# Two query blocks of values at the end of every second slot, in two output banks, in the last ten slots of a sliding-window attention

## The chip, the cores and the metric

The kernel runs on one core of one Trainium2 chip. The metric is the device time of one execution in microseconds (us). The engines are TensorE (PE in the profile; its weight loads are PEld), VectorE (DVE), ScalarE (ACT), GpSimd (POOL) and SyncE (SP), which issues the transfers. TensorE writes only to the accumulators, eight banks of 128 partitions by 512 float32 values.

## The reference

The input x is 2048 tokens of 512 values. It is normalised per token; the result feeds an attention with a window of 256 keys, 32 heads of 16 values, and a mixer with 1792 hidden units; the output joins them.

```python
xn = _layernorm(x)
qkv = (xn @ wqkv).reshape(B, S, 3, H, Dh)            # S 2048, H 32, Dh 16
scores = einsum("bhqd,bhkd->bhqk", q, k) * Dh ** -0.5
mask = (i - j >= 0) & (i - j < 256)
s = (softmax(where(mask, scores, -1e9)) @ v) @ wo
h = gelu(_layernorm(xn) @ w1 + b1)
return x + s * silu(h @ w2 + b2)
```

## The kernel before, in words

**Stages.** The attention stage is followed by a mixer stage that works through the tokens in four chunks of 512. The attention takes the heads four at a time (NQ is 8 groups) and the tokens in 16 blocks of 128, which makes 128 slots, counted by t in the loop at lines 818 to 850. Slot t stands for group t // 16 and block t % 16. Every engine executes its instructions in the order in which this loop records them (the class Ordered, lines 32 to 47), so the loop is a schedule written out by hand.

**One slot**, in the order in which TensorE gets it:

- `prob_block(n, kb, 1)` (lines 547 to 563) makes the scores of key block kb against the three query blocks that can see it, for two of the four heads, with two matmuls of up to 128x384 (`w` is 384, and 256 and 128 for the last two blocks of a group). From slot 116 on they go to the accumulator xy, which was needed until then for running maxima. ScalarE takes the exponential into a buffer `pt`, and GpSimd masks it with two affine selects.
- a first helping of filling matmuls into the banks fb (`fill_in(t, 0)`), and what the plan has for this slot
- `prob_block(n, kb, 0)`, the same for the other two heads, through the accumulator stb
- a second helping of filling matmuls (`fill_in(t, 1)`)
- `pv_step` (lines 568 to 581): the values of one query block, that of the slot before. The query block needs the probabilities of up to three key blocks, so it is 12 matmuls with 17 columns of weights (16 values and the sum), into four groups of rows of `otb`, which is columns 256 to 383 of the second bank of zo (line 194). ScalarE copies it to `oraw`; after four blocks a transfer writes `oraw` to oT_d in memory, from where the mixer stage reads it.

**What fills.** The filling matmuls of the last slots are hidden units of the first chunk (`pair_h`), two at a time in the two row halves of TensorE. `tandem` (lines 439 to 470) spreads them: units 12 and 13 over slots 116, 117, 119 and 120 with the rest in 121, units 2 and 3 over slots 122, 123, 125 and 126 with the rest in 127 (line 745). Slots 118 and 124 get none.

**Buffers.** `pt` comes from a pool of 8 buffers (line 64), two per key block, so four key blocks are held at once. zo is one tile of two banks (line 193). Until slot 115 its columns 0 to 255 take scores for the maxima (`first_scores`, lines 486 to 493); after that only `otb` is in use. The area with the tag `wa` in the pool bigp holds first weights, then an input chunk (`open_y`, line 588), and after the last slot the first hidden units (`activate_first`, line 785).

**After the last slot**, in slot 128 (lines 800 and 801): a hidden unit on all rows (`first_h(0)`), the values of block 127, a second hidden unit (line 856), and then the projections of the mixer stage.

Waits between engines are not written by hand: the recording layer sets them from what instructions read and write, as counts of semaphores.

Of the kernel before, what the change touches and what calls it, by code (L numbers as in the profile page):

```python
# [9 lines left out]
F32 = mybir.dt.float32  # L10
# [8 lines left out]
P = 128  # L19
# [31 lines left out]
def mixer_kernel(ctx, tc, x, wqk, wv, wo, w1, b1, w2, b2, out):  # L51


    nc = SimpleNamespace(**{name: Ordered(tc, name) for name in ("tensor", "vector", "scalar", "gpsimd", "sync")})

    const = ctx.enter_context(tc.tile_pool(name="const", bufs=1))
    bigp = ctx.enter_context(tc.tile_pool(name="bigp", bufs=1))
# [6 lines left out]
    pp = attn.enter_context(tc.tile_pool(name="pp", bufs=8))  # L64
# [95 lines left out]
    def run(steps):  # L160
        for step in steps:
            step()
# [13 lines left out]
    def open_slot(i):  # L176
        slots.append(bigp.tile([P, 2, 2, S], F32R, tag=f"qk{i}", name=f"qk{i}"))
# [5 lines left out]
    oT_d = dram.tile([4, 8, 32, S], F32, name="oT_d")  # L183
# [9 lines left out]
    zo = psum.tile([P, 2, 512], F32, name="zo")  # L193
    otb = zo[:, 1, 256:384]
# [291 lines left out]
    def first_scores(n, qb):  # L486

        slot = slots[n % 2]
        for p in range(2):
            for a in (1, 0):  # L490
                r = slice(64 * a, 64 * a + 64)
                nc.tensor.matmul(zo[:, a, P * p: P * (p + 1)], slot[r, 0, p, P * qb: P * (qb + 1)],
                                 slot[r, 1, p, P * (qb - 2): P * (qb - 1)], start=True, stop=True)

    def max_block(n, qb, ahead=False):

        slot = slots[n % 2]
        if qb % 4 == 0:
            mts[n, qb // 4] = small.tile([P, 2, 2, 4], F32, tag="mt", name=f"mt_{n}_{qb}")
        lo = max(qb - 1, 0)  # L500
        off = 128 * (lo + 1 - qb)
        for p in range(2):
            for a in (1, 0):
                r = slice(64 * a, 64 * a + 64)
                nc.tensor.matmul(xy[:, a, 256 * p + off: 256 * (p + 1)], slot[r, 0, p, P * qb: P * (qb + 1)],
                                 slot[r, 1, p, P * lo: P * (qb + 1)], start=True, stop=True)
        if qb >= 2 and not ahead:
            first_scores(n, qb)
        four = xy.rearrange("q a (p k) -> q a p k", p=2)
        nc.vector.copy_predicated(four[:, :, :, 128:256], mask,  # L510
                                  neg if qb < 2 else zo[:, :, 0:256].rearrange("q a (p k) -> q a p k", p=2))
        nc.vector.tensor_reduce(out=mts[n, qb // 4][:, :, :, qb % 4],
                                in_=four[:, :, :, off:256],
                                axis=AX.X, op=ALU.max, negate=True)

    def max_rows(n, c, t):

        mt = mts.pop((n, c))
        mh = small.tile([P, 2, 2, 2, 4], F32R, tag="mh", name=f"mh_{n}_{c}")
        apart = t >= 0  # L520
        eng = nc.gpsimd if apart else nc.vector
        eng.tensor_copy(mh[:, :, 0], mt)
        eng.tensor_tensor(mh[:, :, 1], mt, mh[:, :, 0].bitcast(F32), op=ALU.subtract)
        mT = small.tile([P, 32], F32, tag="mT", name=f"mT_{n}_{c}")

        def turn_rows():
            nc.vector.transpose(mT, mh.rearrange("p a l i b -> p (a l i b)").bitcast(F32))
        if apart:
            behind(t + 1, turn_rows)
        else:  # L530
            turn_rows()
        t += apart
        rows = mT_d[n, c]
        at(t + 1, nc.sync.dma_start, rows.rearrange("r (i t) -> i r t", i=4), mT)

        def bring_in():
            nc.sync.dma_start(slots[n % 2][3:P:32, 0, :, 512 * c: 512 * (c + 1)].bitcast(F32),
                              rows.rearrange("(h p b) t -> h p (b t)", h=4, p=2))
        if (n, c) == (6, 3):
            among[7, 3] = bring_in  # L540
        else:
            behind(t + 2, bring_in)


    pts = {}

    def prob_block(n, kb, p):
        slot = slots[n % 2]
        w = min(384, S - P * kb)
        pt = pp.tile([P, 2, 384], F32, tag="pt", name=f"pt_{n}_{kb}_{p}")  # L550
        both = xy if p and 16 * n + kb + LEAD >= 16 * NQ else stb[0]
        for a in (1, 0):
            r = slice(64 * a, 64 * a + 64)
            nc.tensor.matmul(both[:, a, 0:w], slot[r, 1, p, P * kb: P * (kb + 1)],
                             slot[r, 0, p, P * kb: P * kb + w], start=True, stop=True)
        nc.scalar.activation(pt[:, :, 0:w], both[:, :, 0:w], AF.Exp, scale=DH ** -0.5)
        nc.gpsimd.affine_select(out=pt[:, :, 0:P], in_=pt[:, :, 0:P], pattern=[[0, 2], [1, P]],
                                compare_op=ALU.is_ge, fill=0.0, base=0, channel_multiplier=-1)
        if w == 384:
            nc.gpsimd.affine_select(out=pt[:, :, 256:384], in_=pt[:, :, 256:384],  # L560
                                    pattern=[[0, 2], [-1, P]], compare_op=ALU.is_gt, fill=0.0,
                                    base=0, channel_multiplier=1)
        pts[(n, kb, p)] = pt


    outs = {}

    def pv_step(n, qb):

        lo = max(qb - 2, 0)  # L570
        for kb in range(lo, qb + 1):
            for j in range(4):
                nc.tensor.matmul(otb[32 * j: 32 * j + DH + 1], vt[:, kb, (4 * n + j) % 16],
                                 pts[n, kb, j // 2][:, j % 2, P * (qb - kb): P * (qb - kb + 1)],
                                 start=(kb == lo), stop=(kb == qb),
                                 skip_group_check=True, tile_position=(0, 32 * j))
        if qb % 4 == 0:
            outs[0] = sgp.tile([P, 512], F32, tag="or", name=f"oraw_{n}_{qb}", bufs=2)
        outs["copy"] = nc.scalar.copy(outs[0][:, P * (qb % 4): P * (qb % 4 + 1)], otb)
        if qb % 4 == 3:  # L580
            (at if n or qb > 7 else behind)(16 * n + qb + 2, nc.sync.dma_start, oT_d[n // 2, n % 2::2, :, P * (qb - 3): P * (qb + 1)], outs[0])


    mlp = {}
# [79 lines left out]
    def at(t, fn, *args):  # L664
        plan.setdefault(t, []).append((fn, args))
# [37 lines left out]
    n, raw = raws["qk"]  # L703
# [107 lines left out]
    def fill_in(t, half):  # L811
        now[:] = t, half
        run(delayed.pop((t, half), ()))
        for fn, args in fills.get((t, half), ()):
            fn(*args)

    end = 16 * NQ
    for t in range(-16, end + 1):
        m = t + LEAD
        if t == -5:  # L820
            open_slot(1)
            for k in range(4):
                at(-4 + k, clear_part, k)
        if 0 <= t < end:
            if t == 0:
                early.close()
                stb.append(attn.enter_context(tc.tile_pool(name="ps_s2", bufs=1, space=PSUM)).tile(
                    [P, 2, 512], F32, name="stb"))
            prob_block(t // 16, t % 16, 1)
        if t >= 0 and m < end:  # L830
            max_block(m // 16, m % 16, m not in IN_PLACE)
        fill_in(t, 0)
        for fn, args in plan.get(t, []):
            fn(*args)
        if 4 <= m < LEAD:
            max_block(0, m)
        if 0 <= t < end:
            prob_block(t // 16, t % 16, 0)
        fill_in(t, 1)
        if 0 <= m < 4:  # L840
            max_block(0, m)
        if t >= 0 and m + 1 < end and (m + 1) % 16 >= 2 and m + 1 not in IN_PLACE:
            first_scores((m + 1) // 16, (m + 1) % 16)
        if t >= 1:
            pv_step((t - 1) // 16, (t - 1) % 16)
        run(lns.get(t, ()))
        if 0 <= m < end and m % 4 == 3:
            max_rows(m // 16, m % 16 // 4, t)
        for fn, args in ends.get(t, []):
            fn(*args)  # L850
# [22 lines left out]
    for f in range(6, NF, 2):  # L873
        t = gp.tile([P, 2, 512], F32, tag="ohl", name=f"hr_{f}", bufs=4)
# [429 lines left out]
```

## Time and profile before

| what | value |
|---|---|
| time, median of 3 runs | 750.63 us (750.46 to 751.04) |
| the profiled execution's own time | 750.88 us |
| its span in the profile | 749.2 us |
| granted TensorE clock | 1.0 |
| the last ten slots, 403.86 to 425.79 us | 21.93 us |

The span is the time from the first to the last instruction that the profile shows; 1.7 us of the execution lie around it. A row of the timeline has the start in us, the duration, the engine, the line, the operation, the tile written and the tiles read, the shape, and how many equal instructions are merged; in brackets stands how long the engine was idle ahead of it and who released it. All instructions have line 43, because one helper records them, so tiles tell them apart: xy and stb are scores, fb is filling, zo the values, pt probabilities, oraw the copy of the values. TensorE overlaps matmuls, so durations in a row overlap; what a piece of work costs is read from start to start.

### The profile page before, as it was taken

How to read it: one execution, taken by the hardware profiler on the slowest of the kernel's cores; microseconds unless marked ns; L12 is line 12 of the kernel's file. 1: busy time of each engine (PE TensorE's matmuls, PEld its weight loads, DVE VectorE, ACT ScalarE, POOL GpSimd, SP SyncE). 2: the span in 40 equal slices, each digit the busy share in tenths (PEclk: the TensorE clock that was granted, in tenths of full speed). 3: DMA queues.
4: the chain of work that ended last, by engine and by line, in shares of the span. 5: the costliest groups of instructions: out<-in, count | busy, mean ns of one | idle time of the engine just before them, and what ended most of it. 6: DMA issues, size and time to landing. Idle time of an engine off the chain costs nothing.

```text
span 749.2 us, 18758 instructions
## 1 busy us (share of the span) xinstructions
PE 733.9 (98%) x7408; PEld 590.4 (79%) x7408; DVE 511.7 (68%) x781; ACT 441.1 (59%) x746; POOL 299.3 (40%) x644
## 2 busy tenths in 40 slices
PE   8999999999999999999999999999999999999997
PEld 7886777777778888777776788888888888888886
DVE  7886777877766778887872648763576765676743
ACT  7757767867667676778877745444463744442001
POOL 7413757767666555767877600120102000001102
PEclk9999999999999999999999999999999999999999
DMA  8633356766555535647724482542012232253611
GB/s 288 191 74 78 84 133 149 201 168 183 152 142 145 144 90 142 162 111 190 200 86 148 133 286 94 165 151 82 31 45 102 93 100 72 70 174 123 222 45 56
DMA packets 56951, 99.40 MB, mean 133 GB/s; under 512 B 11104, under 2 KB 11360, under 8 KB 56864
## 3 DMA queue, kind: packets, MB, share of 16 engines
q1 hardware_dynamic: 56864, 98.21, 45.7%
q8 instruction: 58, 0.95, 0.5%
q14 instruction: 29, 0.24, 0.1%
HBM read 51.39 MB, written 29.62 MB: 108 GB/s over the span
## 4 chain that ended last, share of the span: by engine, by line
PE 89%; ACT 5%; DVE 2%; POOL 2%; issue 1%; DMA 1%; SPq 0%; DVEq 0%; ACTq 0%; POOLq 0%
PE acc L43 20%; PE fb L43 18%; PE zo L43 11%; PE stb L43 9%; PE p L43 9%; PE s L43 6%; PE h L43 6%; PE xy L43 5%; ACT pt L43 4%; PE pv L43 3%; POOL pt L43 1%; DVE xy L43 1%; PE yt L43 1%; DMA x<-in_x_dram 1%; DVE mt L43 0%
## 5 line engine op out<-in xcount | busy, mean ns | idle before, releaser
L43 POOL TENSOR_SCALAR_AFFINE_SELECT pt<-pt 128x256 f32<-128x256 f32 x480 | 193.8, 428 | 132.9 <-ACT pt L43 131.7
L43 ACT ACTIVATE pt<-stb 128x768 f32<-128x768 f32 (+1 forms) x244 | 188.8, 774 | 62.4 <-PE stb L43 54.8
L43 DVE TENSOR_REDUCE mt<-xy 128x4 f32<-128x1024 f32 (+1 forms) x128 | 152.6, 1192 | 4.4
L43 DVE COPY_PREDICATED xy<-upper,zo 128x512 f32<-128x512 int32 x112 | 77.8, 695 | 70.6 <-PE xy L43 63.1
L43 POOL TENSOR_TENSOR xo<-xo,gated 128x512 f32<-128x512 f32 x15 | 20.3, 1358 | 216.8 <-DVE gated L43 192.9
L43 PE MATMUL fb<-xnT,wqb 64*128 64x512 f32 (+1 forms) x684 | 104.8, 397 | 0.3
L43 PE MATMUL zo<-pt,vt 128*17 128x128 f32 x2880 | 103.7, 275 | 0.3 <-POOL pt L43 0.3
L43 PE MATMUL stb<-qk 64*128 64x384 f32 (+1 forms) x488 | 97.2, 393 | 6.2 <-ACT pt L43 4.1
L43 PE MATMUL acc<-w,gh 128*128 128x512 f32 x320 | 98.9, 390 | 0.0
L43 PEld LDWEIGHTS stb<-qk 64*128 64x128 f32 x488 | 45.8, 183 | 51.6 <-ACT pt L43 46.6
L43 PEld LDWEIGHTS zo<-pt,vt 128*17 128x17 f32 x2880 | 67.5, 97 | 15.6 <-issue 6.3
L43 PEld LDWEIGHTS fb<-xnT,wqb 64*128 64x128 f32 (+1 forms) x684 | 64.7, 185 | 11.0 <-DVE pjr L43 1.4
L43 PEld LDWEIGHTS acc<-w,gh 128*128 128x128 f32 x320 | 59.8, 188 | 12.3
L43 PE MATMUL acc<-w,gl 128*128 128x512 f32 x160 | 62.4, 390 | 0.0
L43 PE MATMUL xy<-qk 64*128 64x256 f32 (+2 forms) x536 | 58.4, 291 | 0.2 <-DVE mt L43 0.2
L43 PEld LDWEIGHTS xy<-qk 64*128 64x128 f32 x536 | 46.7, 185 | 6.7 <-issue 3.1
L43 ACT COPY oraw<-zo 128x128 f32<-128x128 f32 x128 | 34.2, 267 | 29.2 <-PE zo L43 28.9
L43 ACT ACTIVATE gated<-acc 128x512 f32<-128x512 f32 x16 | 8.7, 596 | 65.6 <-DVE acc L43 65.6
L43 PE MATMUL s<-wos,ohl 128*128 128x512 f32 (+1 forms) x204 | 44.7, 378 | 0.0
L43 PEld LDWEIGHTS s<-wos,ohl 128*128 128x128 f32 x204 | 36.7, 188 | 7.2 <-DVE gated L43 0.2
L43 PEld LDWEIGHTS zo<-qk 64*128 64x128 f32 x448 | 38.5, 185 | 4.4 <-issue 1.4
L43 ACT COPY p<-p 128x512 f32<-128x512 f32 x21 | 12.3, 586 | 49.7 <-PE p L43 42.3
(195 smaller groups left out, 1241.5 us busy)
## 6 DMA issues: line engine op xcount, KB each, us to landing
qk<-sh SPq DMA_DIRECT2D x128, 128.0 KB
qk<-pjr SPq DMA_DIRECT2D x64, 128.0 KB
oT_d<-oraw SPq DMA_DIRECT2D x32, 256.0 KB
w_d<-in_w_dram SPq DMA_DIRECT2D x14, 512.0 KB
x<-in_x_dram SPq DMA_DIRECT2D x16, 256.0 KB
or<-oT_d SPq DMA_DIRECT2D x16, 256.0 KB
w<-rden_d SPq DMA_DIRECT2D x16, 256.0 KB
xo<-in_x_dram SPq DMA_DIRECT2D x16, 256.0 KB
```

The costliest lines, as they stand in the source:

```text
L43: r = issue(*args, **kwargs)
```

## The change

From slot 118 on, `pv_step` is called in odd slots only, for two query blocks: those of the slot two before and of the slot before (slot 119 does blocks 117 and 118, slot 127 does 125 and 126). Odd blocks use `otb` in the second bank as ever, even blocks the same columns of the first bank. Block 127 stays in slot 128. Because blocks of probabilities are now read up to one slot later, those of key blocks 118 and 123 get a buffer in the area `wa`, outside the pool of 8, one tile for both halves. The transfer of `oraw` is planned for the slot after the one in which the block is computed; so for blocks 116 to 119 and 120 to 123 it moves back by a slot.

```diff
+    TWOS, APART, spare = 118, (118, 123), []
     def prob_block(n, kb, p):
...
-        pt = pp.tile([P, 2, 384], F32, tag="pt", name=f"pt_{n}_{kb}_{p}")
+        if 16 * n + kb in APART:
+            if p:
+                spare.append(bigp.tile([P, 2, 2, 384], F32, tag="wa", name=f"pt_{n}_{kb}"))
+            pt = spare[-1][:, p]
+        else:
+            pt = pp.tile([P, 2, 384], F32, tag="pt", name=f"pt_{n}_{kb}_{p}")
...
-    def pv_step(n, qb):
+    def pv_step(n, qb, t):
+        otb = zo[:, int(t < TWOS or qb % 2), 256:384]
...
         if qb % 4 == 3:
-            (at if n or qb > 7 else behind)(16 * n + qb + 2, nc.sync.dma_start, oT_d[n // 2, n % 2::2, :, P * (qb - 3): P * (qb + 1)], outs[0])
+            (at if n or qb > 7 else behind)(t + 1, nc.sync.dma_start, oT_d[n // 2, n % 2::2, :, P * (qb - 3): P * (qb + 1)], outs[0])
...
-        if t >= 1:
-            pv_step((t - 1) // 16, (t - 1) % 16)
+        for q in range(t - 1, t) if t < TWOS or t == end else range(t - 2, t) if t % 2 else ():
+            if q >= 0:
+                pv_step(q // 16, q % 16, t)
```

## The prediction, as it was put on record

> **What bounds the kernel now.** I read the page first, then the chain of work that ended last, then the last slots of the attention in the timeline of all engines.
>
> ```profile
> span 749.2 us, 18758 instructions
> PE 733.9 (98%) x7408; PEld 590.4 (79%) x7408; DVE 511.7 (68%) x781; ACT 441.1 (59%) x746; POOL 299.3 (40%) x644
> ```
>
> The chain of waits from 425 us to the end, grouped by engine and line:
>
> ```profile
> by line: PE acc L43 47.1%; PE p L43 20.6%; PE s L43 13.6%; PE h L43 13.5%; PE fb L43 1.9%; PE yt L43 1.6%; PE zo L43 0.5%; DVE xo L43 0.3%; DVE gated L43 0.2%; issue 0.0%; PE stb L43 0.0%; DVEq L43 0.0%
> ```
>
> TensorE is busy for 98% of the span. Nearly all of that chain is matmuls that follow each other. So whatever the attention's last slots gain or lose, the end gains or loses, unless something waits there for another engine. The last ten slots are these (start, duration; PE is matmuls, PEld weight loads; each of the 12 matmuls of a block of values has two rows, so x24 is one block):
>
> ```profile
> 401.43 0.85 PE L43 MATMUL fb<-xnT 64*128 64x512 f32 x6
> 402.12 0.34 PE L43 MATMUL stb<-qk 64*128 64x384 f32 x2
> 402.29 0.86 PE L43 MATMUL fb<-xnT 64*128 64x512 f32 x6
> 403.08 0.85 PE L43 MATMUL zo<-pt,vt 128*17 128x128 f32 x24
> 403.86 0.44 PE L43 MATMUL xy<-qk 64*128 64x384 f32 x2
> 404.00 0.27 ACT L43 COPY oraw<-zo 128x128 f32<-128x128 f32 x1 [0.68 <-PE zo L43]
> 404.14 0.34 PE L43 MATMUL stb<-qk 64*128 64x384 f32 x2
> 404.41 0.57 PEld L43 LDWEIGHTS zo<-pt,vt 128*17 128x17 f32 x24 [0.25 <-ACT oraw L43]
> 404.41 0.85 PE L43 MATMUL zo<-pt,vt 128*17 128x128 f32 x24
> 404.43 0.81 ACT L43 ACTIVATE pt<-xy 128x768 f32<-128x768 f32 x1 [0.16 <-PE xy L43]
> 405.29 0.18 PEld L43 LDWEIGHTS xy<-qk 64*128 64x128 f32 x2 [0.31 <-ACT pt L43]
> 405.29 0.44 PE L43 MATMUL xy<-qk 64*128 64x384 f32 x2
> 406.76 0.85 PE L43 MATMUL zo<-pt,vt 128*17 128x128 f32 x24
> 407.54 0.45 PE L43 MATMUL xy<-qk 64*128 64x384 f32 x2
> ...
> 410.02 0.44 PE L43 MATMUL xy<-qk 64*128 64x384 f32 x2
> 411.27 0.85 PE L43 MATMUL zo<-pt,vt 128*17 128x128 f32 x24
> 411.76 0.83 ACT L43 ACTIVATE pt<-stb 128x768 f32<-128x768 f32 x1
> 412.05 0.44 PE L43 MATMUL xy<-qk 64*128 64x384 f32 x2
> 412.47 0.29 ACT L43 COPY oraw<-zo 128x128 f32<-128x128 f32 x1
> 414.76 0.45 PE L43 MATMUL xy<-qk 64*128 64x384 f32 x2
> 416.70 0.85 PE L43 MATMUL zo<-pt,vt 128*17 128x128 f32 x24
> 417.48 0.45 PE L43 MATMUL xy<-qk 64*128 64x384 f32 x2
> 417.62 0.27 ACT L43 COPY oraw<-zo 128x128 f32<-128x128 f32 x1 [0.69 <-PE zo L43]
> 418.03 0.63 PE L43 MATMUL zo<-pt,vt 128*17 128x128 f32 x16
> 418.98 0.41 PE L43 MATMUL zo<-pt,vt 128*17 128x128 f32 x8 [0.31 <-POOL pt L43]
> 419.32 0.44 PE L43 MATMUL xy<-qk 64*128 64x384 f32 x2
> 421.57 0.39 PE L43 MATMUL xy<-qk 64*128 64x256 f32 x2
> 423.95 0.33 PE L43 MATMUL xy<-qk 64*128 64x128 f32 x2
> 425.79 0.50 PE L43 MATMUL fb<-yh,xnT 128*128 128x512 f32 x1
> ```
>
> A slot opens with its scores in xy. The last one, slot 127, is 128 columns wide and opens at 423.95; counting back, slot 118 opens at 403.86, and the first hidden unit follows at 425.79. The ten slots take 21.93 us: 1.43, 2.25, 2.48, 2.03, 2.71, 2.72, 1.84, 2.25, 2.38 and 1.84. TensorE hardly stands still in them. Only slots 118 and 124 have no filling matmuls (fb), and there two waits show. The block of values at 404.41 waits for the copy of the block before (404.00 plus 0.27 is 404.27; the weight load waited 0.25). The scores at 405.29 wait for the exponential that still reads xy (404.43 plus 0.81 is 405.24).
>
> **The change part by part.** Unit prices, from start to start in the rows above: a block of values costs 0.78 (406.76 to 407.54). Six fb rows before scores take 0.69 (401.43 to 402.12), before a block of values 0.79 (402.29 to 403.08), so that turn costs 0.10. Scores after a block take 0.28 (403.86 to 404.14), after fb 0.17 (402.12 to 402.29), so the turn back costs 0.11. A block that follows another and waits for its copy starts 1.33 after it (403.08 to 404.41, and again 416.70 to 418.03): the copy starts 0.92 after the block, lasts 0.27, and 0.14 go to the release and the first weights.
>
> *Even slots lose their block.* In slots 120, 122 and 126 that is 0.78 and one turn of 0.10, 0.88 each: 2.48, 2.71 and 2.38 become 1.60, 1.83 and 1.50. The next scores need the exponential of this slot's first half, which ends 0.57 (403.86 to 404.43) plus 0.81 plus 0.05 after the slot opens, 1.43; it is still covered. Slots 118 and 124 have nothing but scores, and there the removed block was the cover of exactly this wait. So 118 stays at 1.43: its block leaves and an idle TensorE takes its place. Slot 124 falls from 1.84 to 1.43, which is what the wait for GpSimd's mask (418.98) and the copy had cost above the exponential. Sum: 3 times 0.88 plus 0.41, a gain of 3.05.
>
> *Odd slots get a second block.* That is 0.78 in each of the five, and the question on which the forecast hangs: does the second block wait for the copy of the first? The change puts it into the other bank of zo. But zo is one tile, and the instruction list of the changed kernel, built but not run, names a wait. In each pair the first matmul of the second block waits for ScalarE's counter at the copy that was issued just ahead, the first block's; the first block names no such wait any more. Nothing is left to fill that wait, since scores and fb stand before the pair. So the second block starts 1.33 after the first instead of 0.78, and each odd slot grows by 1.33: 6.65. Behind the waiting matmul stand, on TensorE, the rest of the block and the next slot's scores; for those waits ScalarE's next exponential, and for that GpSimd. Bounds of this wait: nothing, if the start could be taken at once (0.78 start to start), and 0.83 rather than 0.55 where the copy comes late on ScalarE. Slot 121 shows that late case: scores stand right ahead of the block, an fb copy and the exponential at 411.76 precede the copy, and it starts 1.20 after the block (411.27 to 412.47) instead of 0.92. The same order stays, so I add 0.28 there once. In slot 127 the exponentials are a third as wide, and I take 0.92. I take 0.55 elsewhere because two rows give 1.33 directly.
>
> *Turns.* Slots 121, 123 and 127 now open after fb or scores and not after a block: 3 times 0.11 gained. Slots 119 and 125 open after a wait, and I give them nothing.
>
> *What costs nothing.* The two blocks of probabilities outside the ring of eight need no wait: that area was last read by slots around 92, and its second use, in slot 123, comes after block 120 of values in slot 121. The other blocks find their ring buffer read a slot earlier, as before; block 120 takes that of block 115, last read by the first block of the pair in slot 119, and its exponential comes after the whole pair. If that failed, an exponential (0.81) would be late once. In the queue of SP the writes of blocks 116 to 119 and 120 to 123 are issued a slot later, the first now behind two writes of h_d. They are read a stage later, behind the last such write, which is not earlier either way. ScalarE gets both copies behind each other, ahead of the next slot's exponential, which needs scores that come after the second block anyway.
>
> Slot by slot this gives 1.43, 3.58, 1.60, 3.53, 1.83, 3.94, 1.43, 3.58, 1.50 and 3.06, together 25.48 against 21.93: **plus 3.55 us** (6.65 plus 0.28, less 3.05 and 0.33).
>
> *Does the rest take it up?* After 425.79 come two hidden units and the projections:
>
> ```profile
> 425.86 2.95 PE fb L43 x12
> 428.81 0.78 PE zo L43 x24
> 429.59 2.97 PE fb L43 x12
> 432.56 5.44 PE acc L43 x24
> ```
>
> All of it is TensorE, and what it reads next is made from the last slots' results, so it shifts with them. I count no refund. The profiled execution took 750.88 us with a span of 749.2; that execution would be at 754.4. It lies 0.25 above the median of 750.63, from which I forecast 754.2.
>
> **The rivals.**
>
> *The banks do stand apart.* If the second block started at once, the five waits of 0.55 and the 0.28 would fall away: 3.55 less 3.03 is plus 0.5, 751.2, not slower by anything that can be told here. It decides from a wait of about 0.2 per pair downward (0.5 and five times 0.2 is 1.5). For it speaks that the blocks write different banks, and that only the copy reads the first. Against it speak the wait in the built list and the two rows in which a block does stand for a copy. On this the Trainium skill, "PSUM — Partial Sum Buffer", section "Summary: rules for kernel authors", says that to read the accumulators while matmuls run, one should take a different bank, and guard by bank. By that rule this rival would be right, with its 751.2; no row of this trace shows a block written beside the copy of another bank of zo, so it neither agrees nor contradicts, and the rule says what the memory allows, not which waits were written into the program. Chance 0.07.
>
> *The copy is late in every pair.* If ScalarE reaches the copy as late as in slot 121 in the other four pairs too, that is 4 times 0.28, and if the turns saved don't show, 3 times 0.10 and 0.33 more: 3.55 plus 1.75, 755.9. For it speaks GpSimd:
>
> ```profile
> 405.30 3.06 POOL L43 TENSOR_SCALAR_AFFINE_SELECT pt<-pt 128x256 f32<-128x256 f32 x8 [1.15 <-ACT pt L43]
> 412.67 10.49 POOL L43 TENSOR_SCALAR_AFFINE_SELECT pt<-pt 128x256 f32<-128x256 f32 x19 [0.43 <-ACT pt L43]
> ```
>
> Its masks take 0.38 each at first and 0.55 later, four to a slot, so 2.2 us a slot; in a pair the second block needs those of the slot just before. Against it: over two slots that is 4.4 us, and the pairs of full width take 5.0 or more in the sum above. Chance 0.12.
>
> *The block was no cover in slots 118 and 124, and the banks stand apart.* Then 118 would save its 0.78 as well, and the sum is about plus 0.5 less 0.8, 750.4: no change that can be told, or a little faster. Against it is the row at 405.29, which names the exponential. Chance 0.02.
>
> **How the numbers follow.** The forecast has 0.79, the late copy 0.12, the separate banks 0.07, the last 0.02. A measurement of this kernel can tell about 0.2%, 1.5 us, from no change, so slower begins at 752.1. The range goes from 752.4, where three of the five waits fall away (1.65) and 0.15 more, to 755.9, the late copy; it leaves out the two rivals below. Slower: 0.79 and 0.12, less 0.01 for a forecast that is off by more, 0.90. Same: 0.08. Faster: 0.02.
>
> **What would show it.** In the profile after, TensorE's weight loads of zo should wait for "ACT oraw" five times for about half a us, in slots 119, 121, 123, 125 and 127, with two blocks 1.33 apart (1.6 in slot 121). The scores of slots 119 and 125 should wait some 0.8 for "ACT pt". The first hidden unit should start at about 429.3 instead of 425.79, and the distance from there to the end should stay. If the pairs stand 0.78 apart the wait was wrong; if slot 118 is shorter than 1.4 the cover was.

## The result and the profile after

The changed kernel takes 754.45 us (median of 6 runs, 753.88 to 754.96); the kernel before, run beside it, 750.62 (750.30 to 751.33). The ratio is 1.0049, 95% interval 1.0036 to 1.0062: slower by half a per cent. The profiled execution took 754.45 us with a span of 752.7, 3.5 more than before. The forecast was 754.2.

The last slots of the changed kernel in TensorE's timeline (start, duration, engine, what, and in brackets the idle time ahead and its releaser; slot 118 opens at 403.87, slot 127 at 426.15):

```profile
403.87 0.44 PE L43 MATMUL xy<-qk 64*128 64x384 f32 x2
404.15 0.34 PE L43 MATMUL stb<-qk 64*128 64x384 f32 x2
405.21 0.44 PE L43 MATMUL xy<-qk 64*128 64x384 f32 x2 [0.73 <-ACT pt L43]
...
406.68 0.85 PE L43 MATMUL zo<-pt,vt 128*17 128x128 f32 x24
407.92 0.85 PE L43 MATMUL zo<-pt,vt 128*17 128x128 f32 x24 [0.38 <-ACT oraw L43]
408.70 0.44 PE L43 MATMUL xy<-qk 64*128 64x384 f32 x2
...
410.31 0.34 PE L43 MATMUL xy<-qk 64*128 64x384 f32 x2
...
411.18 0.35 PE L43 MATMUL stb<-qk 64*128 64x384 f32 x2
411.46 0.85 PE L43 MATMUL zo<-pt,vt 128*17 128x128 f32 x24
413.26 0.85 PE L43 MATMUL zo<-pt,vt 128*17 128x128 f32 x24 [0.96 <-ACT oraw L43]
...
421.17 0.44 PE L43 MATMUL xy<-qk 64*128 64x384 f32 x2 [0.81 <-ACT pt L43]
...
426.15 0.23 PE L43 MATMUL xy<-qk 64*128 64x128 f32 x2
...
428.34 0.85 PE L43 MATMUL zo<-pt,vt 128*17 128x128 f32 x24 [0.39 <-ACT oraw L43]
429.12 0.50 PE L43 MATMUL fb<-yh,xnT 128*128 128x512 f32 x1
```

Every odd slot now ends in two blocks, and the second carries a bracket: it waited for "ACT oraw", the copy of the first. The scores at 405.21 and 421.17 carry the other new wait, for the exponential. The first hidden unit starts at 429.12 instead of 425.79. The waits of TensorE's matmuls between 397 and 430 us, summed (us in total, times, longest):

```profile
PE zo L43 <- ACT oraw L43: 2.5, 5, 1.0
PE xy L43 <- ACT pt L43: 1.5, 2, 0.8
```

The same view of before had neither line; it had one wait of 0.3 us for "POOL pt", and that is gone. ScalarE in slots 120 and 121 of the changed kernel:

```profile
410.05 0.82 ACT L43 ACTIVATE pt<-stb 128x768 f32<-128x768 f32 x1
411.05 0.81 ACT L43 ACTIVATE pt<-xy 128x768 f32<-128x768 f32 x1 [0.19 <-POOL pt L43]
411.76 0.58 ACT L43 COPY hr<-fb 128x512 f32<-128x512 f32 x1
412.23 0.83 ACT L43 ACTIVATE pt<-stb 128x768 f32<-128x768 f32 x1
412.93 0.28 ACT L43 COPY oraw<-zo 128x128 f32<-128x128 f32 x1
```

The copy at 412.93 is the one that the block at 413.26 waits for. From 411.05 on it stands at the end of a chain without a gap: exponential, fb copy, exponential, copy. The block it copies began at 411.46 and ended by the profile at 412.31, 0.62 before the copy began.

Slot by slot, in us from one opening to the next (the two right columns belong to experiments below):

| slot | before | forecast | after | copies after both | three pairs, copies after |
|---|---|---|---|---|---|
| 118 | 1.43 | 1.43 | 1.34 | 1.34 | 1.35 |
| 119 | 2.25 | 3.58 | 3.49 | 2.91 | 2.25 |
| 120 | 2.48 | 1.60 | 1.61 | 1.62 | 1.59 |
| 121 | 2.03 | 3.53 | 3.73 | 2.56 | 2.58 |
| 122 | 2.71 | 1.83 | 1.85 | 1.85 | 1.85 |
| 123 | 2.72 | 3.94 | 3.85 | 3.27 | 3.27 |
| 124 | 1.84 | 1.43 | 1.43 | 1.43 | 1.49 |
| 125 | 2.25 | 3.58 | 3.48 | 2.90 | 2.26 |
| 126 | 2.38 | 1.50 | 1.50 | 1.50 | 1.50 |
| 127 | 1.84 | 3.06 | 2.97 | 2.39 | 2.40 |
| together | 21.93 | 25.48 | 25.25 | 21.77 | 20.54 |

The ten slots are 3.32 longer, the profiled span 3.5.

### The profile page after: what moved, and what is told of

It reads as the page before. It is cut to its first block, busy times and chain, and to the rows that moved or that the text cites. A ratio compares the mean times of both kernels' runs of the same rounds, so it can differ in the third digit from the quotient of the medians.

```text
span 752.7 us, 18759 instructions
## 1 busy us (share of the span) xinstructions
PE 734.5 (98%) x7408; PEld 591.4 (79%) x7408; DVE 511.2 (68%) x781; ACT 440.9 (59%) x746; POOL 298.4 (40%) x644
```

## The experiments

My theory had two prices: the second block waits for the first one's copy, and slots 118 and 124 lose the block that covered the exponential. The change and the first three kernels are the two by two of it: with and without the copy between the blocks, with and without pairs that take the block out of 118 and 124. The fourth kernel takes the block out of these two slots alone. The four ran on one chip, 11 times each; before had 750.77 us there (33 runs).

**Five pairs, copies after both blocks.** The copy and its transfer move out of `pv_step` into a function of their own, which is called after both blocks' matmuls:

```diff
-        for q in range(t - 1, t) if t < TWOS or t == end else range(t - 2, t) if t % 2 else ():
-            if q >= 0:
-                pv_step(q // 16, q % 16, t)
+        done = [q for q in (() if t in SKIP else (t - 2, t - 1) if t - 1 in SKIP else (t - 1,)) if q >= 0]
+        for q in done:
+            pv_step(q // 16, q % 16, t)
+        for q in done:
+            pv_out(q // 16, q % 16, t)
```

with SKIP = (118, 120, 122, 124, 126).

> The five pairs as in the change, but both blocks' matmuls are issued first and both copies after them, so that the second block has no copy ahead of it to wait for. Theory (the wait for the first block's copy is the price): the pairs stand 0.78 us apart instead of 1.23 four times and 1.80 once, 2.85 less; the ten slots 22.4 us instead of 25.25, the time 751.6, still 0.4 to 1.0 above before, because slots 118 and 124 stay uncovered. Rival (two blocks in a row are slow in themselves, or the banks collide): pairs stay over 1 us apart, 754.

Measured: 750.56 us, ratio to before 0.9994 (0.9985 to 1.0003), so no difference from before that can be told. The timeline of all engines at the end of slot 119 of this kernel:

```profile
406.81 1.51 PE L43 MATMUL zo<-pt,vt 128*17 128x128 f32 x48
408.25 0.19 PEld L43 LDWEIGHTS xy<-qk 64*128 64x128 f32 x2 [0.21 <-issue]
408.25 0.44 PE L43 MATMUL xy<-qk 64*128 64x384 f32 x2
408.36 0.19 PEld L43 LDWEIGHTS fb<-xnT 64*128 64x128 f32 x2
408.38 0.43 ACT L43 COPY oraw<-zo 128x128 f32<-128x128 f32 x2 [0.89 <-PE zo L43]
```

The two blocks are one group of 48 rows without a gap, 1.44 from start to the next scores, and both copies follow. The wait was the price, and more of it than expected: a second block right behind the first costs 1.44 less 0.78, 0.66, not another 0.78. The ten slots are 21.77, 3.48 less than in the change, which is all of its loss of 3.32 and a little more. My 751.6 for this kernel was 1.0 too high, 0.6 of it for that reason (four times 0.57 and 1.17 fell away, where I had counted 0.45 or 0.46 and 1.02).

**Three pairs, copies between**: the loop of the change with SKIP = (120, 122, 126), so that 118 and 124 keep their block, and each block still copied ahead of the next.

```diff
+    SKIP = (120, 122, 126)
...
+        for q in () if t in SKIP else (t - 2, t - 1) if t - 1 in SKIP else (t - 1,):
+            if q >= 0:
+                pv_step(q // 16, q % 16, t)
```

> Pairs only at the ends of slots 121, 123 and 127; slots 118 and 124, which have no filling matmuls, keep their block. Copies between, as in the change. Theory (waits and lost cover are two separate prices): slots 118, 119, 124 and 125 as before; 120, 122 and 126 shorter by 0.88 each; 121, 123 and 127 longer by 1.70, 1.13 and 1.13; the ten slots plus 1.3, the time 751.9. Rival (all of the loss comes with the waits, none with the lost cover): three fifths of the 3.8, plus 2.3, 752.9.

Measured: 751.5 us, ratio 1.0009 (1.0000 to 1.0017); the ten slots take 22.78, 0.85 more than before. Slots 121, 123 and 127 have 3.74, 3.85 and 2.98, as in the change, and three waits for the copy remain. I had expected 1.3 more than before: slots 118 and 124 did not stay at 1.43 and 1.84 but took 1.35 and 1.43, with their block in them. The lost cover is a price of its own: two pairs less take 25.25 less 22.78, 2.47, off the slots, more than two waits of 0.57 are worth.

**Three pairs, copies after both**: the first experiment with SKIP = (120, 122, 126).

> Pairs only at the ends of slots 121, 123 and 127, and both copies after both blocks. Theory: neither price is left, only the turns saved (three times 0.10 and three times 0.11): the ten slots 21.3 us, 0.6 less than before, the time 750.0. Rival (pairs cost something of their own, such as later probabilities): no gain, 750.6 or more.

Measured: 749.41 us (749.06 to 749.92, 11 runs), ratio 0.9981 (0.9973 to 0.9990). It is faster than both kernels, 1.4 us below before. TensorE's timeline of it in slots 121 to 124, scores and values alone:

```profile
410.39 1.51 PE L43 MATMUL zo<-pt,vt 128*17 128x128 f32 x48
411.82 0.44 PE L43 MATMUL xy<-qk 64*128 64x384 f32 x2
...
413.67 0.33 PE L43 MATMUL xy<-qk 64*128 64x384 f32 x2
...
415.51 1.50 PE L43 MATMUL zo<-pt,vt 128*17 128x128 f32 x48
416.94 0.44 PE L43 MATMUL xy<-qk 64*128 64x384 f32 x2
...
417.57 0.93 PE L43 MATMUL zo<-pt,vt 128*17 128x128 f32 x24
418.43 0.45 PE L43 MATMUL xy<-qk 64*128 64x384 f32 x2
```

The ten slots take 20.54, 1.39 less than before; I had expected 0.6. Three even slots fall by 0.86 to 0.89, three odd ones rise by 0.55 or 0.56 only, because a block behind a block is 0.12 cheaper than I took it (three times 0.12). Slot 124 has 1.49 instead of 1.84: its block at 417.57 is not broken by the wait of 0.31 for the mask that before had. That I had not put in, nor the 0.08 by which slot 118 is shorter.

**Two pairs, copies after both**: the same with SKIP = (118, 124), the cover alone.

> Pairs only at the ends of slots 119 and 125, so that just slots 118 and 124 lose their block; both copies after both blocks. Theory (the removed block covered the wait for the exponential): slot 118 stays at 1.34 to 1.43, 124 at 1.43, 119 and 125 grow by 0.78 each, the ten slots plus 1.05, the time 751.7. Rival (no cover lost): slots 118 and 124 fall by 0.8 and the ten slots shrink by 0.3 to 0.4, 750.3.

Measured: 751.52 us, ratio 1.0011 (1.0002 to 1.0020); the ten slots 22.76, 0.83 more than before. The scores that follow slots 118 and 124 in its timeline:

```profile
404.47 0.44 PE L43 MATMUL xy<-qk 64*128 64x384 f32 x2
...
405.81 0.45 PE L43 MATMUL xy<-qk 64*128 64x384 f32 x2 [0.73 <-ACT pt L43]
...
418.67 0.45 PE L43 MATMUL xy<-qk 64*128 64x384 f32 x2
...
420.10 0.44 PE L43 MATMUL xy<-qk 64*128 64x384 f32 x2 [0.81 <-ACT pt L43]
```

Without their block the two slots take 1.34 and 1.43, and TensorE stands for 0.73 and 0.81 of it. Of the two blocks of 0.78 that left them only 0.09 and 0.41 are saved, and slots 119 and 125 grow by 0.67 and 0.65. The kernel with three pairs and copies between, which keeps the block in both slots, has 1.35 and 1.43 there. The rival that no cover is lost had 750.3 and falls.

The next three ran on one chip, with before at 750.93 us (7 runs).

**Two tiles.** zo is recorded as two tiles of one bank each; the copies stay between the blocks as in the change. The predicated copy of the maxima reads both banks and had to be split in two.

```diff
-    zo = psum.tile([P, 2, 512], F32, name="zo")
+    zo = [psum.tile([P, 512], F32, name=f"zo{a}") for a in range(2)]
...
-        otb = zo[:, int(t < TWOS or qb % 2), 256:384]
+        otb = zo[int(t < TWOS or qb % 2)][:, 256:384]
```

> The change with zo recorded as two tiles of one bank each; copies stay between the blocks. The predicated copy of the maxima is split in two instructions for it, 112 more on VectorE up to slot 115, so the whole time says little; the ten slots tell. Theory (the wait comes from the recording of zo as one tile): the pairs stand 0.78 us apart although the first block's copy runs beside the second block, ten slots 22.4 us. Rival (the accumulator banks really hold up the second block while ScalarE reads): pairs 1.2 apart, ten slots 25.2.

Measured: the ten slots take 21.79, slot by slot within 0.01 of the five pairs with copies after both; under my 22.4 they are again by five times 0.12. All engines at the end of slot 119 of this kernel:

```profile
416.13 1.50 PE L43 MATMUL zo<-pt,vt 128*17 128x128 f32 x48
417.05 0.27 ACT L43 COPY oraw<-zo 128x128 f32<-128x128 f32 x1 [0.22 <-PE zo L43]
417.56 0.19 PEld L43 LDWEIGHTS xy<-qk 64*128 64x128 f32 x2 [0.21 <-ACT oraw L43]
417.56 0.44 PE L43 MATMUL xy<-qk 64*128 64x384 f32 x2
...
417.70 0.27 ACT L43 COPY oraw<-zo 128x128 f32<-128x128 f32 x1 [0.39 <-PE zo L43]
```

The copy of the first block, 417.05 to 417.32, runs while TensorE writes the second block into the other bank (416.13 to 417.56, without a gap). So the accumulators do allow it, and the wait was written by the recording of both banks as one tile. The whole time of this kernel, 760.42 us (ratio 1.0125, 1.0110 to 1.0140), is another matter: slot 118 opens at 413.31 instead of 403.87, before any pair is reached, with 112 more predicated copies on VectorE.

**Both blocks in the same bank.**

```diff
-        otb = zo[:, int(t < TWOS or qb % 2), 256:384]
+        otb = zo[:, 1, 256:384]
```

> The change with both blocks of a pair in the second bank, as before the change, so that the wait for the copy is needed. Theory (the second bank buys nothing while zo is one tile): the same time as the change, 754.4, ten slots 25.2, pairs 1.23 apart and 1.80 in slot 121. Rival (the second bank saved some of the wait): 1 us or more above the change.

Measured: 753.97 us (ratio to before 1.0043, 1.0027 to 1.0060); the ten slots 25.25, the change's to the hundredth, slot by slot within 0.01. As recorded, the second bank bought nothing.

**The fb copy of slot 121 on VectorE.**

```diff
-        fills.setdefault((t1, 0), []).append((one[2], (fb[0], t1, nc.scalar.copy)))
+        fills.setdefault((t1, 0), []).append((one[2], (fb[0], t1, nc.vector.tensor_copy if t1 == 121 else nc.scalar.copy)))
```

> The change with the fb copy of slot 121 that stands on ScalarE given to VectorE. Theory (the pair in slot 121 stands 1.80 apart because this copy and an exponential hold up the copy of the values in ScalarE's queue): it falls to about 1.3, the other four stay at 1.23, the ten slots 24.75. Rival (the exponential alone, or GpSimd's masks, sets it): it stays over 1.6.

Measured once, 753.08 us; ScalarE in slots 120 and 121:

```profile
409.65 0.81 ACT L43 ACTIVATE pt<-stb 128x768 f32<-128x768 f32 x1
410.65 0.81 ACT L43 ACTIVATE pt<-xy 128x768 f32<-128x768 f32 x1 [0.19 <-POOL pt L43]
411.36 0.80 ACT L43 ACTIVATE pt<-stb 128x768 f32<-128x768 f32 x1
412.05 0.27 ACT L43 COPY oraw<-zo 128x128 f32<-128x128 f32 x1
```

The pair of slot 121 stands 1.32 apart (411.06 and 412.38) instead of 1.80, and the ten slots take 24.77. What made slot 121 worse than the others was ScalarE's queue, with the fb copy as the larger part: 0.48 of the 0.57 that this pair had above the others.

## Why the prediction was right

**The wait for the copy**, the step on which it hung, is there five times, as the list of the built kernel had it. Its size came out near by luck. From block to block I took 1.33, where four pairs have 1.23 or 1.24, and the two rows of before that gave me 1.33 do not show this wait. In slot 121 of before no copy stands between the scores and the block:

```profile
410.59 0.81 ACT L43 ACTIVATE pt<-xy 128x768 f32<-128x768 f32 x1 [0.16 <-POOL pt L43]
411.00 0.34 PE L43 MATMUL stb<-qk 64*128 64x384 f32 x2
411.27 0.57 PEld L43 LDWEIGHTS zo<-pt,vt 128*17 128x17 f32 x24 [0.30 <-issue]
```

The block starts 0.27 after these scores. The blocks at 404.41 and 418.03 start 0.27 after theirs too (404.14 and 417.76). So the copies, which ended at 404.27 and 417.89, held neither of them up, although the profile names the copy ahead of their weight loads. My 1.33 was a block of 0.78 and two scores of 0.28 and 0.27, and these rows did not speak against the rival of separate banks either. In the pairs of the change the distance is the start of the copy 0.92 after the block, its 0.27 and 0.05 to the second block (406.68, 407.60, 407.92). I had 0.92 and 0.27 as well, but 0.14 for the last term. In the other direction, I set the wait at 1.33 less 0.78, 0.55; a second block without the wait costs 0.66, so the wait is worth 0.57. For the sum only the 1.23 counted.

**Slot 121** has 3.73 against 3.53. The late copy was right, its size not. I let the copy start 1.20 after its block, as in before; it started 1.47 after (411.46 to 412.93), and the pair stands 1.80 apart against my 1.61. Of the 0.27, 0.17 is ScalarE: its exponential of the slot's first half began 0.74 after the slot opened (410.31 to 411.05) and in before 0.57 (410.02 to 410.59). The other 0.10 is the block, which stood that much sooner in the slot (1.15 instead of 1.25 after its opening).

**The lost cover** held: 1.34 and 1.43 for slots 118 and 124 against 1.43 and 1.43, with waits of 0.73 and 0.81 where I expected 0.8. By my own sign, a slot 118 under 1.4, the cover would have been wrong. The sign was badly set: slot 118 takes 1.35 with its block too, since its exponential came 0.09 sooner. And the 0.41 that I counted as a gain in slot 124 would have come without taking its block out: with three pairs and copies between, the slot keeps its block and has 1.43 as well. **The turns** held: 1.61, 1.85 and 1.50 for the even slots against 1.60, 1.83 and 1.50. **No refund** came later: from the first hidden unit to the first projection both kernels take 6.60 (425.79 to 432.39 and 429.12 to 435.72), and from there to the end of the span 316.8 and 317.0.

The sum was 3.55; the ten slots have 3.32, the profiled executions 3.57 (754.45 less 750.88), the medians 3.83. The slots account for 3.3 of it; what lies between that and the medians is about the spread of the runs, and I did not settle it.

**The rivals.** That the banks stand apart was right of the chip and wrong of the program: two tiles show the copy beside the block. On this point the Trainium skill's "PSUM — Partial Sum Buffer", "Summary: rules for kernel authors" (take a different bank to read while matmuls run) agrees with the trace, by the copy at 417.05 within the two blocks that start at 416.13. The price of this rival was mis-sized: not plus 0.5 but 0.1 below before (21.79 against 21.93), mostly since I left a second block at 0.78. The rival of a copy that is late in every pair held in slot 121 only. The rival that the removed block was no cover falls with the two waits for the exponential and with slots 118 and 124 of the three pairs, which take with their block what they take without it.

## What to carry to other kernels

Putting results in separate banks freed nothing here while they were recorded as one tile: look in the built program for what the second writer waits for, and issue its matmuls ahead of the first one's copy, or record two tiles. Before a distance between two rows is taken as the price of a wait, compare it with the same rows where nothing has to be waited for: a named releaser is not yet a delay. Before work is moved out of a stretch, ask what it covers there; blocks were worth moving only out of slots that had filling matmuls of their own (three pairs, copies after both, 1.4 us gained), and not out of the two that had none (0.8 lost).

## What the runs showed of the hardware that I had not expected

A block of values behind another costs 0.66 us, a lone one between other work 0.78 and its turns of 0.10 and 0.11. On the turns, the Trainium skill's "TensorEngine Tiling (Array Packing)", "Key Properties", says that a change of tiling mode drains TensorE; the rows agree in so far as they appear where 64-row and 128-row matmuls meet and not between two blocks.

Slot 118 took 1.34 or 1.35 instead of 1.43 in the changed kernel and in all seven experiments, also where it kept its block. Its exponential starts 0.48 after the scores (403.87 to 404.35 in the changed kernel) instead of 0.57 (403.86 to 404.43). ScalarE stood 0.16 ahead of it in before and 0.07 in the changed kernel. There it writes to the new buffer; whether that makes the 0.09 was not tried by itself.
